# A fused block-sorted attention and max-out layer: Strassen's algorithm for the third item's hidden products, one-bank chains for the output groups, and a new order of all steps

## Chip, cores and metric

One core of a Trainium2 chip runs the kernel. The metric is the device time of one execution in microseconds. The profile shows one execution of its own; its span, from the first to the last instruction, is a little shorter than the device time.

## The reference

```python
B, H, S, D = 4, 8, 768, 64;  n_blocks = 8;  block = 96
P = sort_net                                   # (B, H, 8, 8)
for _ in range(5):
    P = np.exp(P - P.max(-1, keepdims=True))
    P = P / (P.sum(-1, keepdims=True) + 1e-09)
    P = P / (P.sum(-2, keepdims=True) + 1e-09)
k_sorted, v_sorted = P applied to the 8 blocks of k and of v
scores = q_b @ k_sorted_b.T / sqrt(D)          # within each block of 96
x = softmax(scores) @ v_sorted_b               # -> (B * S, H * D) = (3072, 512)
g = np.maximum(x @ w1, x @ w2)                 # w1, w2: (512, 1024)
out = g @ w_out                                # (3072, 512) float32
```

"Item" below is one of the four entries of the batch, 0 to 3 (768 tokens of x each).

## The kernel before

**Algebra.** max(a, b) = b + relu(a - b). So the kernel forms W1 - W2 once (in the place of W1, a quarter of its columns at a time), computes h = relu(x (W1 - W2)), and writes out = h W_out + x (W2 W_out). The product W2 W_out (512 x 512, in `wc`) is made once, from W2 transposed (`w2T`). Matmuls take bf16 and accumulate in float32.

**Stages per item.** Sort k (`sort_k`) and v (`sort_v`, `sort_v_pair` for items 1 and 2 together, `sort_v_halved`) by small matmuls on 64 rows of the array; transpose q; scores of 8 blocks at a time (`scores`, 64 rows, exponential on ScalarE into one of six buffers `e`); values (`values`, then a reciprocal and a multiplication on VectorE); transpose x (by matmul for item 0, by a transposing DMA on the SP queue for items 1 to 3); hidden products (`moe_h`, or `HGroup` with Strassen's algorithm); output products (`Group`).

**PSUM.** One pool of four tiles of two banks each. Every step that multiplies takes one of them; an output group holds its tile from its first to its last step.

**Hidden products.** For items 0 to 2, `moe_h` fills one tile per half of the tokens (`ch`) and quarter of the hidden columns (`t`): eight matmuls of 128 x 384 and one ReLU from PSUM, on ScalarE or VectorE. That is 64 matmuls per item; item 0's come in two halves of four (`ha`, `hb`). For item 3, two objects `HGroup` take half of the columns each and make seven products of four matmuls (Winograd's form of Strassen's algorithm): 56 matmuls. Their partial sums are kept in SBUF (steps 0, 2 and 3, a copy), or are added on VectorE (steps 1, 5 and 6) ahead of a ReLU from SBUF; step 4 is a ReLU from PSUM. The sums and differences of x that they need (`x_sums`, tokens X) are made for every item, since the output groups use them as well; those of the weights (`d_sums`, tokens Z, in the place of W2) are made once.

**Output products.** All items use seven products per group. `P` is the group of an item's first two tiles of 128 tokens in each half (12 matmuls of 128 x 256 per step), `U` that of the third tile (6 per step). Sums of g (`g_sums`, tokens G) and of W_out and W2 W_out (`weight_sums`, tokens w) come from VectorE. In `step`, items 0 to 2 alternate between the two banks of their tile: copies at steps 0 and 2, additions of PSUM and SBUF at steps 1, 3, 4, 5 and 6. Item 3 uses `chain`: steps 0, 2, 3 and 4 add up in bank 0 and are copied out after each, steps 1, 5 and 6 use bank 1 and end in additions.

**Order.** The kernel fixes the order of each engine's instructions itself: a list of tokens (`plan`) is run through `token`, and each token issues all its instructions at once, on whichever engines and queues they use. `s2.4` is the scores of item 2, unit 4; `v2.4` the values; `P1.3A` is step 3 of item 1's group P with the evacuation on ScalarE, `D` on VectorE, and `P` as a last letter on GpSimd; `Y3.0.5A` is step 5 of item 3's `HGroup` 0; `k`, `b`, `q`, `x`, `t` are sorting of k and v, transposes of q and x, and a re-ordering copy of v; `T`, `c` and `d` are W2's transposes, W2 W_out and W1 - W2; `lk`, `lq`, `lf`, `lv` load k, q and v through GpSimd's queue. Everything up to the first sorting of k stands ahead of the list: three pieces of v, three of k and four of q for item 0, the recurrence for P, and the weights' loads. Two small writes by GpSimd (`seen`) hold back the weights' loads until P and the first sorted k are there:

```python
    nc.gpsimd.tensor_copy(out=seen[0:G, 0], in_=p_bf[:, NB - 1, NB - 2 :])
    load_w_columns(w2_sb, moe_w2, 0, 1)
    ...
    nc.gpsimd.tensor_copy(out=seen[:, 1], in_=kT[0][:, 0:2])
    load_w_columns(w1_sb, moe_w1, 0, 1)
```

GpSimd's queue also computes two quarters of W1 - W2 (`d0P`, `d1P`), so loads that stand behind those in its order wait for them. At the start TensorE runs 92 matmuls on zeros, then more during the recurrence (`keep_streaming`). In the profile, lines 711 are `moe_h`, 779 `HGroup`, 934 the output products, 581 scores, 609 values, 960 additions, 967 and 969 copies of the output groups.

## Time and profile before

| | |
|---|---|
| device time, median of 3 runs | 159.38 us (159.37 to 160.71) |
| span of the profiled execution | 157.9 us |
| granted TensorE clock, mean | 1.000 |
| line 934, output products | 504 matmuls, 33% of the chain of waits |
| line 711, hidden products of items 0 to 2 | 192 matmuls, 20% of the chain |
| line 779, item 3's hidden products | 56 matmuls |
| exponentials, L597 | 32 on ScalarE, 808 ns each |
| multiplications after the values, L626 | 32 on VectorE, 687 ns each |
| ReLU of hidden products | 20 on ScalarE, 812 ns; 4 on VectorE, 951 ns |
| loads through GpSimd's queue | 13.37 MB written to SBUF, 48.3% of 16 engines' span |
| transposes of x and q, and stores, on hardware queues | 9.84 MB, 26.0% |

Each row of the profile's groups names the line, engine, operation, the tiles written and read, and the shapes; after the count come the total busy time, the mean duration of one in nanoseconds, and the idle time of the engine just before. Matmul durations overlap, so a product's pace is read from how long a run of them takes, not from its mean duration. "Chain of waits" is followed back from the last instruction, at each step to what released it.

### The profile page before, as it was taken

The page shows a single profiled execution, that of the slowest core. Times are in us where ns is not written, and L with a number is a line of the kernel's source. Part 1 is how long each engine was busy: PE and PEld are TensorE (multiplying, and loading weights), DVE is VectorE, ACT ScalarE, POOL GpSimd, SP SyncE. Part 2 cuts the span into 40 slices and gives each one's busy share as a digit, 9 for nine tenths or more (in the row PEclk, how much of TensorE's full clock was granted, in tenths as well). Part 3 has the DMA queues.
Part 4 walks back from the last instruction along what each step waited for, and adds up shares of the span by engine and source line. Part 5 has one row for each costly group of instructions (what it writes and reads, how often), then busy time and mean ns, then how long its engine had stood idle before and what let it go on. Part 6 is the DMA issues. An engine that isn't in the chain of part 4 may idle for free.

```text
span 157.9 us, 5185 instructions
## 1 busy us (share of the span) xinstructions
PE 149.7 (95%) x2260; PEld 115.1 (73%) x2264; DVE 127.1 (81%) x274; ACT 84.4 (53%) x111; POOL 29.3 (19%) x57
## 2 busy tenths in 40 slices
PE   6989799999999999999999999999999999999980
PEld 6839577756467788887676898766689886578870
DVE  4879799939969998892899989979878959799340
ACT  3489795656159993459148700793662106692010
POOL 7969997220100000004300000000000000000000
PEclk9999999999999999999999999999999999999999
DMA  2999999999999999795999995750020719000063
GB/s 40 192 204 199 186 202 205 214 214 216 213 203 217 214 145 192 261 132 174 143 220 211 138 147 115 238 215 0 4 50 4 111 42 395 0 4 0 18 254 129
DMA packets 28918, 23.93 MB, mean 152 GB/s; under 512 B 16672, under 2 KB 24608, under 8 KB 28896
## 3 DMA queue, kind: packets, MB, share of 16 engines
q0 software_dynamic: 9280, 13.37, 48.3%
q1 hardware_dynamic: 19200, 9.84, 26.0%
q8 instruction: 17, 0.28, 0.7%
q10 hardware_dynamic: 416, 0.39, 0.7%
q14 instruction: 5, 0.04, 0.1%
HBM read 26.75 MB, written 6.29 MB: 209 GB/s over the span
## 4 chain that ended last, share of the span: by engine, by line
PE 80%; DMA 9%; DVE 6%; issue 1%; POOL 0%; ACT 0%; DVEq 0%; POOLq 0%
PE out_ps L934 33%; PE h_ps L711 20%; DMA q_raw<-in_q_dram 6%; PE wc_ps L691 4%; PE o_ps L609 4%; DMA v_raw<-in_v_dram 3%; PE hb_ps L779 3%; DVE x L626 3%; PE s_ps L581 3%; PE hq_ps L779 2%; PE k_ps L486 2%; PE v_ps L551 2%; PE tw_ps L672 1%; PE tq_ps L453 1%; DVE o L960 1%
## 5 line engine op out<-in xcount | busy, mean ns | idle before, releaser
L711 PE MATMUL h_ps<-xT,w_sb 128*128 128x384 bf16 x192 | 33.9, 326 | 0.1
L597 ACT ACTIVATE e<-s_ps 96x768 bf16<-96x768 f32 x32 | 23.8, 808 | 13.3 <-PE s_ps L581 13.1
L711 PEld LDWEIGHTS <-w_sb 128*128 128x128 bf16 x192 | 17.8, 98 | 10.8
L725 ACT ACTIVATE g<-h_ps 128x768 bf16<-128x768 f32 x20 | 16.0, 812 | 15.1 <-PE h_ps L711 14.9
L626 DVE TENSOR_TENSOR x<-o_ps,rs 96x512 bf16<-96x512 f32 x32 | 22.0, 687 | 1.1
L934 PEld LDWEIGHTS <-g 128*128 128x128 bf16 x192 | 18.3, 98 | 2.3
L934 PEld LDWEIGHTS <-sums_g 128*128 128x128 bf16 x144 | 13.7, 98 | 1.7
L960 DVE TENSOR_TENSOR o<-out_ps,a 128x512 f32<-128x512 f32 (+1 forms) x20 | 11.0, 550 | 3.4 <-PE out_ps L934 2.1
L960 DVE TENSOR_TENSOR o<-out_ps,o 128x512 f32<-128x512 f32 (+1 forms) x16 | 8.8, 555 | 5.6 <-PE out_ps L934 5.5
L934 PE MATMUL out_ps<-wo_sb,g 128*128 128x256 bf16 x96 | 13.1, 273 | 0.0
L609 PEld LDWEIGHTS <-e 96*128 96x128 bf16 x256 | 10.8, 98 | 2.4 <-DVE x L626 0.2
L609 PE MATMUL o_ps<-v_sb,e 96*128 96x65 bf16 x256 | 12.1, 193 | 0.1
L934 PE MATMUL out_ps<-w2T,sums_x 128*128 128x256 bf16 x72 | 11.8, 273 | 0.0
L109 ACT CAST v_sb<-v_ps 96x1024 bf16<-96x1024 f32 x10 | 9.7, 1027 | 0.4 <-PE v_ps L528 0.4
L934 PEld LDWEIGHTS <-sums_x 128*128 128x128 bf16 x96 | 9.0, 98 | 1.2
L581 PE MATMUL s_ps<-qT,kT 64*128 64x96 bf16 x256 | 8.9, 204 | 0.7 <-issue 0.4
L620 DVE RECIPROCAL rs<-o_ps 96x8 f32<-96x8 f32 x32 | 6.3, 197 | 3.4 <-PE o_ps L609 3.2
L581 PEld LDWEIGHTS <-kT 64*128 64x128 bf16 x256 | 6.3, 94 | 3.6 <-issue 2.6
L109 ACT CAST kT<-k_ps 128x1024 bf16<-128x1024 f32 x7 | 7.0, 1013 | 3.4 <-PE k_ps L486 3.4
L969 ACT COPY o<-out_ps 128x512 f32<-128x512 f32 (+1 forms) x7 | 3.5, 503 | 9.7 <-PE out_ps L934 9.7
L111 DVE CAST v_sb<-v_ps 96x1024 bf16<-96x1024 f32 x6 | 7.3, 1216 | 1.2 <-PE v_ps L528 0.8
L779 PEld LDWEIGHTS <-w_sb 128*128 128x128 bf16 x56 | 5.5, 98 | 3.5
(135 smaller groups left out, 272.4 us busy)
## 6 DMA issues: line engine op xcount, KB each, us to landing
out_dram<-o SPq DMA_DIRECT2D x10, 512.0 KB, 3.3
v_raw<-in_v_dram POOLq DMA_DIRECT2D x8, 384.0 KB, 15.5
k_raw<-in_k_dram POOLq DMA_DIRECT2D x3, 768.0 KB, 19.3
w_sb<-in_moe_w_dram POOLq DMA_DIRECT2D x4, 256.0 KB, 6.3
w_sb<-in_moe_w_dram POOLq DMA_DIRECT2D x2, 512.0 KB, 9.0
wo_sb<-in_moe_w_out_dram POOLq DMA_DIRECT2D x2, 512.0 KB, 12.6
v_raw<-in_v_dram POOLq DMA_DIRECT2D x3, 256.0 KB, 5.4
k_raw<-in_k_dram POOLq DMA_DIRECT2D x3, 256.0 KB, 7.9
```

Source lines behind the costliest of these rows:

```text
L109: nc.scalar.copy(out=out_ap, in_=in_ap)
L111: nc.vector.tensor_copy(out=out_ap, in_=in_ap)
L581: nc.tensor.matmul(ps[:, h2 * 512 + ii * 128 : h2 * 512 + ii * 128 + BLK], kT[b][rows, (hp * 8 + i) * BLK : (hp * 8 + i) * BLK + 128], rhs ...
L597: nc.scalar.activation(out=e_out, in_=src, func=AF.Exp, scale=scale)
L609: nc.tensor.matmul(ps[:, h2 * 512 + ii * 65 : h2 * 512 + (ii + 1) * 65], e[:, (h2 * 4 + ii) * BLK : (h2 * 4 + ii) * BLK + 128], v_sb[:, m0 ...
L626: nc.vector.tensor_tensor(out=x, in0=ov[:, :, :, 0:D], in1=rs.to_broadcast([BLK, 2, 4, D]), op=ALU.mult,)
L691: nc.tensor.matmul(ps[:, 0:512], w2T[:, fb, dmt * 128 : (dmt + 1) * 128], wo_sb[:, fb, :], start=(fb == 0), stop=(fb == NFB - 1),)
L711: nc.tensor.matmul(h_ps[ch, t][:, m * 512 : m * 512 + TCH], w1_sb[:, hp, fb * 128 : (fb + 1) * 128], xT[:, b % 2, ch, hp % 2, hp // 2, :], ...
L725: nc.scalar.activation(out=g, in_=src, func=AF.Relu)
L779: nc.tensor.matmul(ps[:, m * 512 : m * 512 + TCH], w[:, k, c : c + 128], x[:, k], start=new and k == 0, stop=k == 1, skip_group_check=True,)
L934: ins = nc.tensor.matmul(self.ps[:, bank * 512 + p * NW : bank * 512 + (p + 1) * NW], left(self.b, lw, k, ti * 128), right(rw, k), start=n ...
L960: ins = nc.vector.tensor_tensor(out=self.part(ch, half), in0=self.by_tile(self.bank(n)), in1=other, op=ALU.add)
```

## The change

- Item 2's hidden products are made by two `HGroup`s, as item 3's. In the list, eight `h2` tokens give way to fourteen `Y2` tokens.
- All output groups use `chain`; the alternating form is gone. Items 0 to 2 store the first half of the tokens after step 4 and the second after step 6.
- All steps, those ahead of the list too, become tokens of one list, with a new order. `f` is filling on TensorE, `I` the identity, `lw`, `lk0`, `lq0` the pieces of item 0's v, k and q, `a` a load of weights (1: W1, 2: W2, by quarters of columns; 3: W_out, by halves), `S` a round of the recurrence, `m` masks, `g` and `J` selections, `D` the first block diagonals, `tv` the re-ordering of item 0's v. The weights' loads are no longer held back by the `seen` writes, and W1 and W2 come in seven pieces in another order, W_out between them.
- The buffers of the exponentials are handed out in the order in which they come free, not in turn.

```diff
...
@@ -177,24 +180,20 @@
     w2_sb = big.tile([128, HP, DFF], BF16, tag="w2", name="w2_sb")
     wo_sb = big.tile([128, NFB, DMODEL], BF16, tag="wo", name="wo_sb")
 
-    def load_w(dst, src):
+    def load_w(dst, src, i):
         s = src.rearrange("(t p) f -> p t f", p=128)
         n = s.shape[1] // 2
-        for i in range(2):
-            nc.gpsimd.dma_start(
-                out=dst[:, i * n : (i + 1) * n, :], in_=s[:, i * n : (i + 1) * n, :]
-            )
+        nc.gpsimd.dma_start(
+            out=dst[:, i * n : (i + 1) * n, :], in_=s[:, i * n : (i + 1) * n, :]
+        )
 
     def load_w_columns(dst, src, t0, t1):
         s = src.rearrange("(t p) f -> p t f", p=128)
         c = slice(t0 * DFF // 4, t1 * DFF // 4)
         nc.gpsimd.dma_start(out=dst[:, :, c], in_=s[:, :, c])
 
-    load_v(0, 3)
+    load_v(0, 3, which=0)
     ident = const.tile([128, 128], BF16, tag="ident", name="ident")
-    make_identity(nc, ident)
-    load_k(0)
-    load_q(0)
 
     id64 = const.tile([128, 64], FP32, tag="id64", name="id64")
     maskJ = const.tile([128, 7, NB], FP32, tag="maskJ", name="maskJ")
...
@@ -562,7 +563,7 @@
             eng=eng,
         )
 
-    e_tiles, x_tiles, e_next = {}, {}, [0]
+    e_tiles, x_tiles, e_free = {}, {}, list(e_bufs)
 
     def scores(b, u, n=0):
         ih, hp = divmod(u, HP)
...
-        e = e_bufs[e_next[0] % NE]
-        e_next[0] += 1
+        e = e_free.pop(0)
         src = ps[0:BLK].rearrange("p (t f) -> p t f", t=8)[:, :, 0:BLK]
         if b == 1:
             e_out = e[:, 0 : 8 * BLK].rearrange("p (t ch c) -> p t ch c", t=8, ch=2)
         e = e_tiles.pop((b, u))
+        e_free.append(e)
         m0 = (b % 2) * 64
         ps = ps_f32("o_ps")
         keep_streaming(ps, n)
@@ -991,21 +993,29 @@
             elif at == 4:
                 self.product(0, 4, "b22", False)
                 self.copy(self.part(0, 1), 0, eng)
-                self.store(0)
+                if last or len(self.tiles) > 1:
+                    self.store(0)
             elif at == 5:
                 self.product(1, 3, 3, True)
                 self.add(1, 1, 1, self.part(1, 1), [self.third], eng)
-                self.store(1, NW)
+                if last:
+                    self.store(1, NW)
             else:
                 self.product(1, "a22", 4, False)
                 self.add(1, 0, 1, self.part(1, 0), [self.second], eng)
-                self.store(1, 0, NW, nc.scalar)
+                if last:
+                    self.store(1, 0, NW, nc.scalar)
+                elif len(self.tiles) > 1:
+                    self.store(1)
+                else:
+                    nc.sync.dma_start(
+                        out=out[self.b * S : (self.b + 1) * S, :].rearrange(
+                            "(c t p) n -> p c t n", c=2, p=128
+                        )[:, :, self.tiles[0], :],
+                        in_=self.both,
+                    )
 
         def step(self, at, eng):
-            if at and self.b == B - 1:
-                self.chain(at, eng)
-                return
-            a = self.by_tile(self.a) if at else None
             if at == 0:
                 n = len(self.tiles)
                 self.ps = ps_f32("out_ps")
...
                 self.product(0, "a11", "b11", True)
                 self.first = self.copy(self.by_tile(self.a), 0, eng)
-            elif at == 1:
-                self.product(1, 2, 2, True)
-                self.second = self.add(1, 0, 1, a, [self.first], eng)
-            elif at == 2:
-                self.product(0, "a12", "b21", False)
-                self.copy(self.part(0, 0), 0, eng)
-            elif at == 3:
-                self.product(1, 1, 1, False)
-                self.third = self.add(0, 1, 1, a, [self.first], eng)
-            elif at == 4:
-                self.product(0, 3, 3, True)
-                self.fourth = self.add(1, 1, 0, self.part(0, 1), [self.third], eng)
-            elif at == 5:
-                self.product(1, 4, "b22", False)
-                self.fifth = self.add(0, 1, 1, a, [self.first, self.fourth], eng)
-                if len(self.tiles) > 1:
-                    self.store(0)
             else:
-                self.product(0, "a22", 4, False)
-                self.add(
-                    1, 0, 0, self.part(1, 0), [self.first, self.second, self.fifth], eng, True
-                )
-                if len(self.tiles) > 1:
-                    self.store(1)
-                else:
...
-
-    first, second, both = slice(0, 64), slice(64, 128), slice(0, 128)
+                self.chain(at, eng)
+
+    def spread_masks():
+        for c, n, m in [(2, 2, 0), (4, 3, 1)]:
+            nc.gpsimd.tensor_copy(
+                out=maskJ[:, c : c + n],
+                in_=maskJ[:, m].to_broadcast([128, NB, n]).transpose([0, 2, 1]),
+            )
+
+    first = slice(0, 64)
+    weights = {
+        1: (load_w_columns, w1_sb, moe_w1),
+        2: (load_w_columns, w2_sb, moe_w2),
+        3: (load_w, wo_sb, moe_w_out),
+    }
     keep_streaming(ps_f32("fill_ps"), 92 * 118, most=118)
-    for it in range(5):
-        sinkhorn(it)
-        if it < 3:
-            masks(it)
-        if it == 2:
-            turn_v(first, "A", 0, 18)
-        if it == 3:
-            turn_v(first, "A", 18, 36)
-    for c, n, m in [(2, 2, 0), (4, 3, 1)]:
-        nc.gpsimd.tensor_copy(
-            out=maskJ[:, c : c + n],
-            in_=maskJ[:, m].to_broadcast([128, NB, n]).transpose([0, 2, 1]),
-        )
-    turn_v(first, "A", 36, 56)
-    turn_v(first, "A", 56, 80)
-    block_diagonals_first()
-    seen = const.tile([128, 2, 2], BF16, tag="seen", name="seen")
-    nc.gpsimd.tensor_copy(out=seen[0:G, 0], in_=p_bf[:, NB - 1, NB - 2 :])
-    load_w_columns(w2_sb, moe_w2, 0, 1)
-    selections(1)
-    selections(2)
-    turn_v(first, "D", 80, 96)
-
-    sort_k(0, 0, 640, "A")
-    nc.gpsimd.tensor_copy(out=seen[:, 1], in_=kT[0][:, 0:2])
-    load_w_columns(w1_sb, moe_w1, 0, 1)
-    load_w_columns(w2_sb, moe_w2, 1, 2)
-    selections(3)
-    load_w_columns(w1_sb, moe_w1, 1, 2)
-    load_w_columns(w2_sb, moe_w2, 2, 4)
-    load_w_columns(w1_sb, moe_w1, 2, 4)
-    load_w(wo_sb, moe_w_out)
 
     def token(text):
 
...
@@ -1163,29 +1144,30 @@
     landed = const.tile([128, 4], BF16, tag="landed", name="landed")
     plan = [
         """
-        k0.1D k0.2A b0.2A b0.0D b0.3A q0.0D q0.1D s0.4 b0.1D s0.5 s0.6 s0.7 lk1 v0.4 s0.0 v0.6
-        s0.3 v0.5 d0P s0.1 T1D s0.2 d1P v0.7 x0.2A v0.1 T0A x0.3D ha0.1.0 v0.0 ha0.1.1 v0.2
-        hb0.1.1A lq1 v0.3 lf1 hb0.1.0A x0.0D T3D d3D T2A d2D x0.1A ha0.0.1 ha0.0.0 ha0.1.3
-        hb0.1.3A X0.1D X0.2D hb0.0.1A ha0.1.2 hb0.0.0A B0 ha0.0.2 hb0.1.2A w0.3D G0.0.1D w0.1D
-        hb0.0.2A c0A G0.0.2D X0.4D k1.0D k1.1A lf3 lf2 k1.2D X0.3D G0.1.1D c3D G0.1.2D c2D q1.0A
-        q1.1D c1A s1.4 w0.2D w1.1D lf0 G0.1.3D G0.0.3D s1.1 s1.2 ha0.0.3 hb0.0.3A t1.3D t1.2D
-        w1.2D P0.0A s1.3 t1.1D t1.0D s1.7 s1.6 G0.0.4D w0.4D P0.1D b2.1A G0.1.4D lq2 lk2 b2.3A
-        P0.2A p2.0D w1.3D b2.2D p2.1D b2.4A w1.4D b2.7A P0.3D q2.0 q2.1 b2.5A b2.6D b2.0A P0.4D
-        v1.4 v1.1 P0.5D s1.0 s1.5 v1.7 P0.6D v1.6 v1.5 U0.0A U0.1D k2.0A x1.2 k2.2A v1.0 U0.2A
-        x1.3 v1.2 U0.3D x1.0 v1.3 k2.1A lk3 k3.2D U0.4D s2.7 s2.3 s2.6 U0.5D x1.1 U0.6D s2.2
-        s2.5 s2.0 h1.1.1A v2.7 h1.1.3D v2.3 v2.0 y1 h1.0.1D h1.1.2D h1.1.0A G1.1.1D lq3 v2.6
-        k3.0D G1.0.1D k3.1A G1.1.3D h1.0.0A G1.0.2D h1.0.2A lv0 G1.0.3D s2.4 p3.0A s2.1 X1.1D
-        P1.0A p3.1D q3.0 X1.2D h1.0.3A G1.0.4D G1.1.2D q3.1 X1.3D Z1D x2.3 X1.4D v2.5 P1.1D lv1
-        U1.0A v2.1 P1.2D v2.4 P1.3D G1.1.4D P1.4D U1.1D v2.2 t3.0D U1.2D U1.3D t3.1D x2.2 x2.1
-        P1.5D U1.4D t3.2D s3.4 s3.5 x2.0 P1.6D s3.7 s3.3 t3.3D U1.5D U1.6D b3.0A b3.1D s3.2
-        h2.1.3A b3.2D Z2D b3.3A h2.1.0A X2.1D X2.2D h2.1.1D G2.1.1D Z4D X2.4D h2.1.2A v3.3
-        G2.0.1D v3.4 h2.0.0A h2.0.1A G2.1.2D h2.0.3A v3.2 x3.1 v3.7 h2.0.2A G2.0.2D v3.5 P2.0A
-        X2.3D s3.1 G2.1.4D s3.0 s3.6 P2.1D U2.0D U2.1D v3.6 G2.1.3D v3.0 G2.0.3D x3.3 U2.2D
-        P2.2A x3.2 U2.3D v3.1 Z3D P2.3D G2.0.4D x3.0 P2.4D U2.4D U2.5D P2.5D P2.6D U2.6D X3.1D
-        X3.2D X3.3D Y3.1.0A Y3.0.0A Y3.1.1D Y3.1.2A Y3.0.2A X3.4D Y3.0.1D Y3.1.3A Y3.0.3A
-        Y3.0.5A Y3.1.5D Y3.1.4A Y3.0.4A Y3.0.6A Y3.1.6A G3.0.1D G3.0.2D G3.1.1D G3.1.2D P3.0A
-        U3.0D P3.1D P3.2A G3.1.4D G3.0.3D G3.0.4D U3.1D U3.2A G3.1.3D P3.3D P3.5D U3.3A P3.4A
-        P3.6D U3.5D U3.4D U3.6D
+        f4 lw1 I1 lk0.0 S0 m0 S1 lw2 m1 lk0.2 lk0.1 lq0.0 S2 m2 J1 tv0.18A S3 tv36.56A S4 tv56.80A
+        lq0.1 D0 tv18.36A tv80.96D k0.0A lq0.3 k0.2D k0.1A lq0.2 b0.3D b0.1A q0.0D g1 a1.0.1 a2.0.1
+        a2.2.3 m3 b0.0A b0.2D s0.5 q0.1D s0.1 s0.4 v0.5 s0.7 v0.1 s0.6 v0.4 s0.0 a2.1.2 a1.2.4 v0.7
+        s0.3 T0D x0.2A v0.6 s0.2 a2.3.4 T2D T1A a3.1 v0.0 x0.3D d0P ha0.1.0 d2D a3.0 v0.3 d3D x0.0A
+        lf1 g3 X0.1D hb0.1.0A ha0.1.2 hb0.1.2A v0.2 g2 B0 a1.1.2 lk1 ha0.0.0 ha0.1.3 x0.1A T3D
+        G0.0.1D hb0.1.3D lq1 X0.3D X0.2D lf2 ha0.0.2 c3D w0.1D X0.4D d1P c0D w0.3D c2D ha0.0.1
+        hb0.0.0D hb0.0.2D ha0.1.1 hb0.1.1A hb0.0.1D k1.0A k1.2A k1.1A q1.0A G0.1.1D G0.0.2D G0.1.2D
+        lf0 G0.0.4D G0.0.3D q1.1D c1A w0.2D ha0.0.3 t1.0D s1.1 G0.1.3D lf3 s1.2 t1.1D s1.3 hb0.0.3D
+        t1.3D lq2 w1.1D P0.0A s1.6 s1.5 s1.4 t1.2D w1.2D lk3 P0.1D b2.1D w1.3D p2.0D b2.5A P0.2A
+        b2.7A b2.6D b2.4A w0.4D P0.3A b2.2A G0.1.4D b2.3A b2.0D P0.5D P0.4A p2.1D w1.4D lk2 v1.4
+        q2.0 v1.5 P0.6D U0.0A q2.1 v1.3 x1.2 s1.7 s1.0 Z1D U0.1D k2.1A v1.7 U0.2A v1.6 v1.0 v1.2
+        U0.3A x1.3 U0.5D x1.1 k2.2A k2.0A v1.1 x1.0 U0.4A U0.6D s2.3 s2.4 s2.5 h1.1.2A h1.1.0D X1.1D
+        s2.1 s2.6 X1.3D X1.2D h1.1.3A y1 v2.4 v2.3 Z3D h1.1.1A G1.1.1D Z2D k3.2A s2.7 X1.4D G1.0.1D
+        lv0 Z4D s2.2 h1.0.0A lq3 lv1 h1.0.1D v2.5 G1.0.2D G1.1.2D h1.0.2A G1.0.3D U1.0A v2.1 v2.2
+        h1.0.3A G1.1.3D U1.2A v2.6 U1.1D p3.0A k3.1A G1.0.4D k3.0D s2.0 p3.1D U1.3A U1.5D q3.0
+        G1.1.4D v2.7 q3.1 P1.0A t3.0D U1.4D x2.3 x2.1 t3.1D U1.6D t3.2D v2.0 t3.3D P1.2A P1.1D x2.0
+        x2.2 P1.3A s3.7 b3.0D b3.1A P1.4A s3.0 b3.2D b3.3A P1.5D Y2.0.0A X2.1D s3.6 X2.2D X2.3D s3.2
+        X2.4D P1.6D Y2.0.2A Y2.0.1D s3.3 v3.7 Y2.0.3A Y2.0.5D Y2.1.0A v3.2 Y2.0.4A Y2.0.6D Y2.1.2A
+        Y2.1.1D s3.4 v3.3 Y2.1.3A Y2.1.5A U2.0A v3.6 Y2.1.4A G2.0.1D Y2.1.6A G2.0.3D G2.0.2D P2.0A
+        s3.1 G2.1.1D s3.5 G2.1.2D G2.1.3D U2.1D x3.1 x3.3 P2.1D v3.4 U2.2A G2.1.4D G2.0.4D P2.2A
+        v3.1 v3.0 x3.0 U2.3A U2.5D U2.4A v3.5 x3.2 U2.6D P2.3D P2.5D X3.1D Y3.1.0A X3.2D Y3.0.0A
+        Y3.0.1A P2.4A P2.6D X3.3D X3.4D Y3.0.2A Y3.1.2A Y3.1.1D Y3.0.3A Y3.1.3A Y3.0.5A Y3.0.4D
+        Y3.1.5D Y3.1.4A Y3.0.6A U3.0A Y3.1.6A G3.0.1D G3.0.2D G3.1.1D P3.0A G3.1.2D G3.0.3D G3.1.3D
+        G3.0.4D P3.1D P3.2A U3.2A U3.1D G3.1.4D U3.3A P3.3D P3.5D P3.4A P3.6D U3.5D U3.4A U3.6D
         """,
     ]
     for part in plan:

```

## Prediction

> **What bounds the kernel now.** I read the page first, then the chain of waits in order of time, then busy time by stretch, then the groups by shape.
>
> ```profile
> span 157.9 us, 5185 instructions
> ...
> PE 149.7 (95%) x2260; PEld 115.1 (73%) x2264; DVE 127.1 (81%) x274; ACT 84.4 (53%) x111; POOL 29.3 (19%) x57
> ...
> DMA  2999999999999999795999995750020719000063
> ```
>
> TensorE is busy 95% of the span. The DMA engines are full for about the first 50 us and have room after that.
>
> ```profile
> 7.59 8.98 DMA q_raw<-in_q_dram
> 16.61 0.55 PE tq_ps L433 x12
> ...
> 48.80 1.31 PE out_ps L934 x12
> 50.11 0.62 PE s_ps L581 x24
> 50.72 1.42 PE out_ps L934 x12
> ...
> 139.61 13.86 PE out_ps L934 x126
> 153.50 0.42 DVE o L960
> ```
>
> The columns are start, duration and what. The chain waits for the last part of item 0's q until 16.6, is nearly all TensorE from there to 153.5, and ends with one addition and a store (4.4 us to 157.9). Two prices come from here. Twelve output products take 1.31 us, but 1.42 where they follow a score or sorting product (64 rows instead of 128): each change between the two kinds costs about 0.1 us. And item 3's output groups, which already accumulate in one bank, ran 126 products in 13.86 us, 0.110 each, so they lost next to nothing.
>
> ```profile
> 11.50:24.50 13.00, 11.70 (x350) 9.87 (x349) 11.48 (x21) 11.42 (x15) 12.72 (x20) 1.00 1.33 196
> 24.50:46.40 21.90, 21.74 (x338) 13.85 (x339) 17.55 (x35) 10.91 (x13) 4.61 (x8) 1.00 1.11 212
> 90.00:130.50 40.50, 40.50 (x498) 32.44 (x495) 34.67 (x68) 14.81 (x20) 0.00 (x0) 1.00 0.44 97
> 130.50:139.60 9.10, 9.10 (x59) 5.51 (x57) 7.85 (x14) 6.48 (x9) 0.00 (x0) 1.00 0.42 163
> 139.60:153.50 13.90, 13.86 (x127) 12.09 (x124) 9.43 (x19) 4.35 (x8) 0.00 (x0) 1.00 0.18 66
> ```
>
> After each stretch and its length stand PE, PEld, DVE, ACT and POOL, then clock, DMA share and GB/s. TensorE has holes only before 24.5. From 46.4 on a product saved is time saved, if VectorE (86% in 90 to 130.5) and ScalarE keep up.
>
> ```profile
> L711 PE MATMUL h_ps<-xT,w_sb 128*128 128x384 bf16 x192 | 33.9, 326 | 0.1
> L779 PE MATMUL hb_ps<-sums_x,w_sb 128*128 128x384 bf16 x24 | 4.4, 326 | 0.0
> L798 DVE TENSOR_TENSOR g<-hq_ps,hs 128x768 bf16<-128x768 f32 x4 | 3.6, 953 | 0.9 <-ACT hs L791 0.8 <-PE hq_ps L779 0.2
> L969 ACT COPY o<-out_ps 128x512 f32<-128x512 f32 x4 | 2.4, 597 | 6.1 <-PE out_ps L934 6.1
> L960 DVE TENSOR_TENSOR o<-out_ps,a 128x512 f32<-128x512 f32 x10 | 6.8, 683 | 2.1 <-ACT e L597 1.2 <-PE out_ps L934 0.9
> ```
>
> The mean of a product (326 ns) counts its way through the array; the pace is 8 in 1.30 us in the chain, 0.163 each.
>
> **Item 2's hidden products.** Eight groups of eight products (64) become two Strassen groups of 28 (56): 8 x 0.163 = **1.30 us** less on TensorE, in a stretch without holes. Evacuation grows. Gone are seven ReLUs on ScalarE (7 x 0.81) and one on VectorE (0.95). New are six copies (0.80) and two ReLUs (0.80) from PSUM on ScalarE, six additions on VectorE (0.95, L798), four ReLUs on VectorE (0.36, L802) and two on ScalarE (0.84, L800). ScalarE goes from 5.7 to 8.1 us, VectorE from 0.95 to 7.2. The sums of x and weights that the products read were already made for items 2 and 3.
>
> Around them VectorE has, by my count over the new list from Y2.0.6 to U2.1, 9.5 us of work against 8.3 of TensorE; the stretch before it has 7.8 against 8.6. The cover is that earlier slack and the 4.2 us of other products between the last hidden product (Y2.1.6) and the first that reads its sums (U2.2). Without the cover the cost is 9.5 - 8.3 = 1.2; I take 0.2.
>
> **Output groups of items 0 to 2 in one chain.** Their 378 products stay (0.109 each). Of seven evacuations per group, steps 3 and 4 turn from additions into copies, which ScalarE can take. Counting letters in the lists, items 0 to 2 go from 16 wide and 18 narrow evacuations on VectorE (0.69 and 0.42) to 10 and 10: 18.6 to 11.1 us. ScalarE goes from 5 and 3 (0.59 and 0.37) to 11 and 11: 4.1 to 10.6. With item 2's hidden work VectorE is about even and ScalarE gains some 9 us on 84, so neither becomes the bound on average.
>
> The price is waits. Before, a product returned to a bank two steps later, and the lists put 0.9 to 5.3 us of other products between. Now step 3 waits for the copy of step 2, step 4 for that of step 3 and step 6 for the addition of step 5. The closest pairs in the new list have between them: U2 steps 3 to 4, 0.66 us; U0 steps 2 to 3, 0.73; P1 steps 3 to 4, 0.82; U2 steps 5 to 6, 0.90; P0 steps 2 to 3, 0.99; P1 steps 5 to 6, 1.10. The need is a copy (0.37 or 0.59), or an addition (0.42 or 0.69), and some 0.2 of handing over: 0.6 to 0.9. The nearest row is U3 steps 5 to 6 in the trace before: 0.66 between, one addition ahead in VectorE's queue, and TensorE waited 0.09 at 152.4. Six such waits give 0.5, and only half the pairs are as tight: I take **0.3**, with 0 and, if each finds one full evacuation ahead (0.8, an exponential), 6 x 0.8 = 4.8 as ends. Behind a waiting product stands everything on TensorE. [...]
>
> **The list.** Over the whole list the changes between 64-row and 128-row products rise from 51 to 55, 33 to 35 of them after item 1's first scores: **+0.2** there, the other two inside the front below.
>
> In the front the order of loads changes: weights follow q at once (two writes by GpSimd that held them back are gone), w_out now stands before the second quarter of W1, and the masks and selections move among the loads. The recurrence that ends with p at 11.1 us is unchanged, and so is the place of k and q in the queue (2.36 MB at about 0.2 MB per us, last q near 16.5). New is that only half of q is needed for the first three scores: q's first half is evacuated near 16.4 instead of 16.87, its scores follow, and the values' VectorE work can start near 18.7 instead of 19.78. That is a gain of 1.1 us at 19. By the first hidden product it is 0.4 in time (24.1 for 24.48) plus 0.7 of products done earlier.
>
> Part of it is lost again, because two steps then need late loads. Before the second quarter of W1 come 2.36 MB of v, k and q, 1.57 MB of W1 and W2, 1.05 of w_out and 0.39 of v; with its own 0.26 it lands at about 35. GpSimd's difference d1P (2.15, L233) then ends near 37.0, and ha0.0.1 is due on TensorE at 36.7. Behind d1P on GpSimd wait five loads, of which v's pieces are due on VectorE only after 46. Item 1's q lands near 42.4, due 42.6. I take 0.3 of waits, so item 1's first scores stand at 46.75 with 0.65 us more work done than at 46.4 before: **-0.3**, bounds -0.9 (nothing waits) and +0.7 (both loads a microsecond later; the first delay then hides the second). [...]
>
> Of the older waits after 46.4 (holes of 0.1 to 0.3 us beside the changes of kind, about 0.9 in all) the new list may lose some; I take -0.3, ends -0.9 and 0. The end (U3.5, U3.4, U3.6, last addition, store) is as before: 4.4 us.
>
> **Sum.** -1.30 + 0.2 + 0.3 + 0.2 - 0.3 - 0.3 = -1.2: the span goes from 157.9 to 156.7. The median of the runs, 159.38, is 1.48 above the span, which I keep: **158.2 us**. The forecast's own band is 157.2 to 159.2.
>
> **Rivals.** *The single bank* (slower): chain waits find ScalarE's queue full. For: from item 1's first scores to P0.3 the new list gives ScalarE 9.5 us beside 8.9 of TensorE, and P0.2 to P0.4 stand among sorting copies of 1.0 each. Against: the list before had 10.7 beside 8.2 there without losing more than 0.6. It decides from 1.2 us beyond my 0.3, about 0.25 per tight pair; at 4.8 instead of 0.3 the time is 162.7, at half of it 160.3.
>
> *The loads*: the front gives back its gain, +0.7 instead of -0.3: 159.2. For: the DMA engines are full there. Against: bytes up to item 1 are the same.
>
> *Not what it says*: VectorE in item 2's stretch takes back the saved 1.3 (1.2 instead of 0.2, and nothing from older waits): 158.2 + 1.0 + 0.3 = 159.5. For: 9.5 against 8.3. Against: item 3's same steps ran with no hole.
>
> *Everything fits*: front -0.9, chain 0, older waits -0.9, item 2 0: -1.3 + 0.2 - 0.9 - 0.9 = -2.9, so 156.5.
>
> **Chances.** One per cent (157.8 and 161.0) is about what a measurement of this kernel can tell from no change, as its three runs spread 0.8%. Forecast 0.46 (0.16 of it under 157.8), everything fits 0.27 (all under), loads or item 2 0.11 (within), single bank 0.16 (0.13 above 161.0, 0.03 within). Faster 0.16 + 0.27 = 0.43; within 0.30 + 0.11 + 0.03 = 0.44; slower 0.13. Range 156.7 to 160.6: it leaves out the far end of everything fits (about 0.05) and of the single bank (about 0.14).
>
> **What would show it.** L711 falls to 128 products and L779 rises to 112, at 0.163. Right: item 2's stretch and the output groups show 12 products in 1.31 to 1.42 and no waits named out_ps from L960 or L969 over 0.3 us; first hidden product near 24.1, item 1's first scores near 46.8, last product near 152.3. Wrong: holes before wide or narrow output products among sorting copies (single bank); TensorE waiting for w_sb, L233 or q_raw between 31 and 44 (loads); idle TensorE with VectorE solid in item 2's stretch.

## The result, and the profile after

The changed kernel takes 164.67 us (median of 4 runs, 164.12 to 167.66) where the kernel before takes 159.52 in the same job: 1.029 times, with a 95% interval of 1.023 to 1.034. It is slower, by about 5 us where 1.2 less were predicted. The ratio leaves out the run of 167.66, in which the granted clock was lower in stretches (0.979 in the mean), and unless it is said otherwise the readings below are of another execution (e0 below), span 161.8, clock 1.00.

The page's totals and its groups, to be held against those of before:

```profile
PE 150.6 (93%) x2253; PEld 115.6 (71%) x2256; DVE 128.9 (80%) x270; ACT 92.0 (57%) x127; POOL 29.3 (18%) x56
...
DMA  3999999999999920999799839993022062700046
...
L712 PE MATMUL h_ps<-xT,w_sb 128*128 128x384 bf16 x128 | 23.1, 326 | 1.8 <-DMA xT<-x 1.4
L970 ACT COPY o<-out_ps 128x256 f32<-128x256 f32 (+1 forms) x21 | 10.0, 474 | 18.3 <-PE out_ps L935 16.7
```

The edit did what it says: 128 ordinary hidden products are left of 192, and the output groups' evacuations have moved to ScalarE (84.4 to 92.0 us busy). TensorE's busy share fell from 95 to 93%, though it has less to do, and the DMA row has a new gap in its 15th and 16th slice (2 and 0, 56.6 to 64.7 us; 9 and 9 stood there before). What TensorE waits for from 46.4 on, in us in total, times and longest:

```profile
PE h_ps L712 <- DMA xT<-x: 1.4, 1, 1.4
PE tq_ps L454 <- issue: 1.4, 1, 1.4
PE hb_ps L780 <- DMA xT<-x: 1.0, 1, 1.0
PE out_ps L935 <- ACT e L597: 0.3, 1, 0.3
```

(The second began at 45.5 and ended inside the stretch.) None is an output product waiting for an addition or a copy. Two are the transposes of x by DMA. The chain of waits, in order of time, shows how they hang together (start, duration, what):

```profile
45.52 1.36 issue
...
73.19 3.92 DMA xT<-x
...
80.24 10.68 DMA v_dc<-in_q_dram
...
91.70 1.47 ACT q_pair L413
...
102.03 5.07 DMA xT<-x
```

Item 1's x is transposed late; GpSimd's small copy of it (token y1) holds v3's pieces and q3's load; q3 lands at 90.9, is rearranged, is transposed on SyncE, and only behind that come x's transposes for item 2, for which its hidden products wait. (Between 93 and 102 the listed chain follows ScalarE and TensorE. The last part of item 2's x was computed by 100.5; SyncE was with x's first two transposes until 101.3 and with a store until 101.9, and took up the last two at 102.0.) SyncE's timeline shows the queue, first in the kernel before, then here:

```profile
56.62 3.86 SPq L422 DMA_TRANSPOSE qT<-q_pair  x2
...
65.50 5.67 SPq L639 DMA_TRANSPOSE xT<-x  x4
...
87.38 4.12 SPq L422 DMA_TRANSPOSE qT<-q_pair  x2
91.59 5.90 SPq L639 DMA_TRANSPOSE xT<-x  x3
```

```profile
63.60 0.41 SPq L975 DMA_DIRECT2D out_dram<-o  x1
64.11 1.81 SPq L423 DMA_TRANSPOSE qT<-q_pair  x1
65.98 1.13 SPq L975 DMA_DIRECT2D out_dram<-o  x1
67.16 2.49 SPq L423 DMA_TRANSPOSE qT<-q_pair  x1
69.69 6.95 SPq L640 DMA_TRANSPOSE xT<-x  x4
...
94.57 3.30 SPq L423 DMA_TRANSPOSE qT<-q_pair  x2
97.98 3.32 SPq L640 DMA_TRANSPOSE xT<-x  x2
```

In this execution a transposing DMA holds SyncE for 1.2 to 2.5 us. Before, q2's two went at 56.6 to 60.5; now they start 7.5 us later (its second rearrangement, p2.1, runs on VectorE at 62.4 instead of 56.0), and SyncE works almost without a pause from 63.6 to 77.3.

To find where the 5 us arise I counted, for each execution, the matmuls that had started by a time, each at the pace of its shape (distance to the next: an output product 0.109, a hidden product 0.163; the small ones, scores and transposes among them, some hundredths), fill left out. The table has this work done, less that of before, in us. The paces of the small products can be taken in more than one way, which moves the entries by some 0.2, and a few matmul records are missing (at most 4 in 2260).

```
by time (us)         24.5   46.4     73     78    104    108    115    150
e0  changed          -1.3   -2.3   -2.0   -3.8   -4.3   -5.4   -5.6   -6.1
e6  front of before  -0.5   -0.4   -1.6   -2.5   -2.3   -3.4   -3.9   -4.1
e9  q3 load ahead     0.0    0.2   -0.6   -0.8   -1.1   -1.9   -2.4   -2.8
e10 x2 early         -0.2    0.4    0.4    0.2    0.6    0.2    0.1   -0.2
e11 x2 early, plain   0.2    0.7    1.2    1.1    1.1    0.7    0.6    0.2
e5  before, chain     0.2    0.1   -1.4   -1.6   -5.7   -6.8   -6.4   -9.7
```

(The other rows are experiments below.) In the changed kernel 2.3 us are lost up to 46.4, where it stands in the middle of the stop in item 1's q transposes (45.5 to 46.9); at 47.0, behind the stop, it is 2.7. Of these 0.7 come back by 73, 1.8 go between 73 and 78, 1.1 between 104 and 108, and 1.2 in small pieces. Against that stand 1.3 us of products fewer: 6.1 - 1.3 = 4.8, about the 5.0 us by which the last product is late (158.2 for 153.2).

### The profile page after: what moved, and what is told of

Read it like the earlier page. It is cut to its first block, busy times and chain, and to the rows that moved or that the text cites. A ratio compares the mean times of both kernels' runs of the same rounds, so it can differ in the third digit from the quotient of the medians.

```text
span 165.8 us, 5166 instructions
## 1 busy us (share of the span) xinstructions
PE 152.5 (92%) x2253; PEld 115.3 (70%) x2256; DVE 129.4 (78%) x270; ACT 91.8 (55%) x127; POOL 29.5 (18%) x56
## 4 chain that ended last, share of the span: by engine, by line
PE 73%; DMA 11%; DVE 8%; issue 3%; POOL 2%; ACT 1%; POOLq 0%
PE out_ps L935 32%; PE h_ps L712 10%; PE hb_ps L780 7%; DMA xT<-x 6%; DMA k_raw<-in_k_dram 5%; PE hq_ps L780 5%; PE o_ps L610 4%; PE s_ps L582 4%; PE k_ps L487 4%; PE wc_ps L692 2%; DVE wt_early L853 1%; ACT e L597 1%; PE v_ps L552 1%; PE v_ps L508 1%; DVE sums_x L865 1%
## 5 line engine op out<-in xcount | busy, mean ns | idle before, releaser
L597 ACT ACTIVATE e<-s_ps 96x768 bf16<-96x768 f32 x32 | 24.4, 806 | 2.8 <-PE s_ps L582 2.4
L712 PE MATMUL h_ps<-xT,w_sb 128*128 128x384 bf16 x128 | 23.5, 329 | 2.2 <-DMA xT<-x 1.4
L970 ACT COPY o<-out_ps 128x256 f32<-128x256 f32 (+1 forms) x21 | 10.0, 474 | 18.4 <-PE out_ps L935 16.7
L712 PEld LDWEIGHTS <-w_sb 128*128 128x128 bf16 x128 | 12.0, 99 | 10.6 <-issue 3.7
L780 PEld LDWEIGHTS <-w_sb 128*128 128x128 bf16 x112 | 10.7, 99 | 9.0 <-DMA xT<-x 2.6
L726 ACT ACTIVATE g<-h_ps 128x768 bf16<-128x768 f32 x9 | 7.3, 812 | 15.8 <-PE h_ps L712 15.8
L728 DVE TENSOR_SCALAR g<-h_ps 128x768 bf16<-128x768 f32 x7 | 6.6, 955 | 7.5 <-PE h_ps L712 7.5
L109 ACT CAST kT<-k_ps 128x1024 bf16<-128x1024 f32 x10 | 9.7, 1013 | 1.4 <-PE k_ps L487 1.4
L111 DVE CAST v_sb<-v_ps 96x1024 bf16<-96x1024 f32 x7 | 8.5, 1218 | 2.0 <-PE v_ps L529 1.7
L780 PE MATMUL hb_ps<-sums_x,w_sb 128*128 128x384 bf16 x48 | 9.4, 326 | 0.0
L109 ACT CAST v_sb<-v_ps 96x1024 bf16<-96x1024 f32 x9 | 8.9, 1019 | 0.3 <-PE v_ps L508 0.3
```

Source lines behind the costliest of these rows:

```text
L109: nc.scalar.copy(out=out_ap, in_=in_ap)
L111: nc.vector.tensor_copy(out=out_ap, in_=in_ap)
L597: nc.scalar.activation(out=e_out, in_=src, func=AF.Exp, scale=scale)
L712: nc.tensor.matmul(h_ps[ch, t][:, m * 512 : m * 512 + TCH], w1_sb[:, hp, fb * 128 : (fb + 1) * 128], xT[:, b % 2, ch, hp % 2, hp // 2, :], ...
L726: nc.scalar.activation(out=g, in_=src, func=AF.Relu)
L780: nc.tensor.matmul(ps[:, m * 512 : m * 512 + TCH], w[:, k, c : c + 128], x[:, k], start=new and k == 0, stop=k == 1, skip_group_check=True,)
```

## The experiments

All ratios are against runs of the kernel before in the same job; the span is that of the profiled execution. A hole of TensorE is given below from the start of one product to the start of the next, less the pace of the first; the lists of waits count from the modelled end of a product, and so have some 0.2 less.

```
run                   median us   ratio  95% interval     span
e0 changed, again       163.49   1.0250  1.0165-1.0335   161.8
e1 c1 between           163.93   1.0252  1.0214-1.0290   161.5
e2 q2 first             163.49   1.0211  1.0158-1.0265   161.5
e3 U stores on ScalarE  166.39   1.0396  1.0337-1.0454   163.4
e4 item 2 plain         166.26   1.0363  1.0285-1.0442   164.9
e5 before, chain        168.64   1.0515  1.0455-1.0576   166.6
e6 front of before      161.56   1.0110  1.0020-1.0200   159.4
e7 DMA order            176.95   1.0984  1.0875-1.1092   174.8
e8 q2 early             160.76   1.0044  1.0004-1.0083   159.5
e9 q3 load ahead        160.69   1.0062  1.0025-1.0100   158.8
e10 x2 early            158.36   0.9929  0.9896-0.9962   156.1
e11 x2 early, plain     159.26   0.9979  0.9955-1.0003   157.0
f1 weights held         163.68   1.0189  1.0087-1.0291   162.0
f2 W1 ahead of w_out    164.59   1.0263  1.0198-1.0327   162.2
```

**The changed kernel again** (e0), no edit:

> The changed kernel as it is, for a second profile. If the time goes where its first profile has it, TensorE shows the same four holes: before the hidden products near 38 us (0.8), inside item 1's transposes of q near 45 (1.9), before item 1's hidden products near 75 (1.8), and before item 2's near 107 (2.5), with TensorE at half its pace for about 3 us behind one or more of the long ones. If it were the chains in one bank, holes of 0.1 to 0.8 us would stand before output products (line 935) all through 53 to 135. Time 164 to 165 us.

It is the base for what follows. The four holes are there, somewhat shorter than in the first execution (0.44, 1.53, 1.58 and 0.25, 1.19 us), and the half pace that the expectation names is not.

**A w product between item 1's k and q** (e1):

```diff
- k1.0A k1.2A k1.1A q1.0A ... q1.1D c1A w0.2D
+ k1.0A k1.2A k1.1A c1A q1.0A ... q1.1D w0.2D
```

> One step of W2 W_out (token c1) is moved from behind item 1's q transposes to between its k sorting and its q transposes. [...] With eight wide products (1.7 us, 32 instructions) in between, the hole shrinks from 1.9 to under 0.4 us, the half pace behind it goes, and the time falls by 1.5 to 3.5 us, to 161 to 163. Rival, q of item 1 comes late: the transposes go on at the same moment as before (46.9 us), the hole only moves in front of them, and the time stays within 0.5 us of 164.4.

The hole of 1.53 us inside q1's transposes shrank to 0.23, and the scores after them then waited 0.95 for VectorE's copy of q1. By 50 us TensorE was some 0.7 us further than in e0, by 78 only some 0.3, and the time is the same: what was won in front was waited for at x's transposes. Why TensorE stops at this place no run shows.

**q2's transposes a few steps earlier** (e2):

```diff
- b2.0D P0.5D P0.4A p2.1D w1.4D lk2 v1.4 q2.0 v1.5 P0.6D U0.0A q2.1 v1.3
+ b2.0D p2.1D q2.0 q2.1 P0.5D P0.4A w1.4D lk2 v1.4 v1.5 P0.6D U0.0A v1.3
```

> Item 2's second pairing copy and its two q transposes (p2.1, q2.0, q2.1) are moved ahead of P0.5 and P0.4, so that they stand on the SP queue before item 0's two stores instead of between and behind them. Theory: SP takes 1.3 to 3.0 us for each transposing DMA and works in order, so item 1's x transposes were held up by it, not by their data; the hole before item 1's hidden products near 75 us falls from 1.8 to under 0.5 us and the time by 1 to 2 us. Rival, the values on VectorE are what x waits for: the hole stays at 1.5 us or more and the time within 0.5 us.

The wait ahead of item 1's hidden products fell from 1.58 and 0.25 us to 0.47, the one ahead of item 2's rose from 1.19 to 1.98. The chain's first link moved; its last, q3 and x2, stayed where they were.

**U's stores on ScalarE's queue** (e3):

```diff
- nc.sync.dma_start(
+ nc.scalar.dma_start(
      out=out[self.b * S : (self.b + 1) * S, :]...
```

> The 512 KB store of each U group of items 0 to 2 is issued on ScalarE's queue instead of SP's. Theory: item 1's U store stands on SP directly before item 2's third x transpose (103.5 and 104.1 us) and moves ahead of it in the same ring, so that this transpose lands 5.4 us after its issue instead of 3.0. Without it the hole before item 2's hidden products near 107 falls from 2.5 to under 0.7 us, the half pace behind it goes, and the time falls by 2 to 3.5 us, to 161 to 162.5. Rival, x of item 2 is late because its last values are: the hole stays over 2 us and the time within 0.5 us.

Slower. SyncE went straight from q3's transposes to all four of x2's, and they ended at 106.4 all the same (105.1 in e0); the holes grew in sum (1.41 and 0.67; 1.98). So it is not the store between x2's transposes that makes them late. Why it lost another 1.6 us of span I did not follow up.

**Item 2's hidden products in ordinary groups** (e4); Strassen's third use is undone, all else stays:

```diff
- Y2.0.0A ... Y2.0.2A Y2.0.1D ... Y2.0.3A Y2.0.5D Y2.1.0A ... (14 steps)
+ h2.0.0A ... h2.0.2A ... h2.1.0A h2.1.2D h2.0.1A ... (8 groups)
```

> Item 2's hidden products go back to eight ordinary groups of eight; everything else as changed. TensorE then has 1.3 us more of products (8 x 0.163) and VectorE and ScalarE have less to evacuate. If Strassen's saving is real and the loss lies in the waits ahead (x and q transposes, front), the waits stay and the saving goes: about 1.0 to 1.3 us slower than the changed kernel, some 164.7. If the new evacuations had eaten the saving, the time is the changed kernel's within 0.3 us or below it, 163.2 to 163.7. If the wait for x's transposes is what counts in that stretch, the wait before item 2's hidden products stays between 1 and 2.5 us in both.

The wait for x2 stayed (1.50 us) and the products added came on top, which speaks for a real saving and a loss that lies elsewhere. Its size is better read from e10 and e11, since e4's execution also had TensorE at half pace for 3.4 us (granted clock 0.5 from 48.2 to 51.6) after the hole in q1's transposes (1.89 here).

**The kernel before, with the one-bank chain alone** (e5), its own list and letters (the conditions on the stores inside `chain`, as in the changed kernel, are left out here):

```diff
-            if at and self.b == B - 1:
+            if at:
                 self.chain(at, eng)
```

> The kernel before with its own list; only the output groups of items 0 to 2 follow the one-bank chain, engine letters as they stood (steps 3 and 4 become copies on the same engine). If the chain's waits cost little, as the changed kernel's trace has it (no hole before output products above 0.5 us), the time is 159.5 to 161.0. If the single bank is the cause (rival), the list that leaves less between the chained steps shows it: 162 or more, with TensorE waiting for out_ps from the addition's or copy's line.

The rival's end, 8.8 us slower, and with the rival's mark. TensorE's waits from 46.4 on:

```profile
PE out_ps L934 <- DVE o L967: 4.9, 5, 1.6
PE out_ps L934 <- DVE o L960: 2.1, 4, 0.8
PE out_ps L934 <- ACT o L969: 0.6, 1, 0.6
PE out_ps L934 <- ACT g L725: 0.6, 1, 0.6
```

Of these 8.2 us, 7.6 are waits for copies and additions of the output groups (`o`), 0.6 is one for a ReLU (`g`). The old list puts one chained step behind the next; the new list does not, and shows none of these waits. So the chain needs its list: my forecast that its waits are cheap held for this list, not for the chain.

**The front of before** (e6): loads, selections and steps of before up to item 1's first scores but one, then the changed list less what is done.

```diff
- f4 lw1 I1 lk0.0 S0 m0 S1 lw2 ... a3.1 ... a1.1.2 lk1 ... lf0 G0.0.4D
+ (list of before, up to) lf0 G0.1.3D G0.0.3D
  s1.1 ...
```

> The list of before up to item 1's first scores but one (46 us there), loads and selections as before; after that the changed list, less what is already done. By the work that TensorE had done at 46.4 us the changed front is about 2.9 us behind. If TensorE's work binds from there on, this gains 2.5 to 3 us: 160.5 to 161. If the middle is bound by the chain q2's rearrangement, transposes on SyncE, loads of q3, transposes of x (each waiting for the one before), the gain is only as much as that chain starts earlier: 161.5 to 163, with the waits before item 1's and item 2's hidden products as long as or longer than before (1.5 and 1.2 us).

The front is worth 1.9 us of median (the two jobs' ratios give 2.2, the two profiled spans 2.4). Of the 2.3 us of work gained behind the stop, at 47, 2.0 are left at 150; the waits at 72.0 (1.60 and 0.25), 92.5 (0.44) and 106.5 (0.92) stay.

**q2 and q3 early in the changed kernel** (e7), q3's load as soon as its place is free:

```diff
- p2.0D b2.5A ... b2.0D P0.5D P0.4A p2.1D w1.4D lk2 ... h1.0.0A lq3 lv1
+ p2.0D p2.1D q2.0 q2.1 b2.5A ... b2.0D lq3 P0.5D P0.4A w1.4D lk2 ... h1.0.0A lv1
```

> Changed kernel; q2's second rearrangement and its transposes right after the first (about 4 us earlier on VectorE), and q3's load issued as soon as its place is free, instead of behind the wait for item 1's x and q2's transposes and behind a piece of v3. If the chain x1's transposes, q3's load, q3's rearrangement, q3's transposes, x2's transposes makes the two holes at 73.8 (1.58 and 0.25) and 105.8 (1.19) and the one at 94.4 (0.47), 2 to 3.3 us go: 160.5 to 161.5. If the 16 DMA engines are simply full there, the transposes get longer beside q3's load and the time stays within 0.7 us of 163.5.

A mistake of placing. GpSimd stood at q3's load until 62.3, and behind it stood k2's load, due on TensorE at 68.4: a hole of 9.6 us (k_raw, issued at 63.21, landed at 78.03). It says nothing of the rest.

**q2 early, with the front of before** (e8):

```diff
- p2.0D b2.5A ... P0.4A p2.1D w1.4D lk2 v1.4 q2.0 v1.5 P0.6D U0.0A q2.1
+ p2.0D p2.1D q2.0 q2.1 b2.5A ... P0.4A w1.4D lk2 v1.4 v1.5 P0.6D U0.0A
```

> The kernel with the front of before (161.56 us), and q2's second rearrangement with both transposes of q2 right after the first rearrangement, instead of some 5 us later; no load is moved. If the wait before item 1's hidden products (1.60 and 0.25 us at 72 to 74) is the queue on SyncE (q2's transposes, then x's, each 1.2 to 3 us of issue), it goes: q2's transposes start near 57 instead of 62.3, and 1.5 to 2 us are gained: about 159.7; item 1's x landing earlier lets v3 and q3 load earlier, so the wait before item 2's hidden products (0.92) shrinks too, if that chain is what makes it. If x's transposes are slow only because the DMA engines are full then, they start earlier and end as late as before: 161.3 to 161.8.

The wait ahead of item 1's hidden products is gone. x's transposes started 2.9 us earlier than in e6 (65.1 for 68.0) but took 9.0 us instead of 6.9, so GpSimd's loads behind them moved by 0.9 only, and the wait ahead of item 2's hidden products rose to 1.69. Half of each expectation held.

**q3's load ahead of v3's, and cover for x2** (e9):

```diff
- lv0 Z4D s2.2 h1.0.0A lq3 lv1
+ lq3 Z4D s2.2 h1.0.0A lv0 lv1
- P1.5D Y2.0.0A X2.1D s3.6 X2.2D X2.3D s3.2 X2.4D P1.6D Y2.0.2A Y2.0.1D
+ P1.5D s3.6 P1.6D Y2.0.0A X2.1D X2.2D s3.2 X2.3D X2.4D Y2.0.1D Y2.0.2A
```

> As the run with q2 early, and besides q3's load ahead of v3's first piece on GpSimd, and item 1's last output products (12, 1.3 us) ahead of item 2's first hidden products instead of behind them. By the chain q3's load, its rearrangement on ScalarE, its transposes, x2's transposes on SyncE, the 0.44 at 92.5 and the 0.92 at 106.5 go: 1.0 to 1.4 us less than the run with q2 early, about 158.4, which is below the kernel before (159.8). If TensorE's waits there come from VectorE (v3's turning, sums of x), not from the transposes, nothing is gained: 159.5 to 160.

No gain in time. The waits at 98.8 and 103.3 (0.27, 1.69) became 0.74 at 102.9, where P1.6 stands one score behind P1.5 and waits for its addition (the tight pair is mine), and 0.42 twice, where item 2's products wait for sums of x that VectorE could form only when x2 was there.

**x2 early** (e10):

```diff
- U1.0A v2.1 v2.2 h1.0.3A G1.1.3D U1.2A v2.6 U1.1D p3.0A ... p3.1D U1.3A U1.5D q3.0
-   G1.1.4D v2.7 q3.1 P1.0A t3.0D U1.4D x2.3 x2.1 ... v2.0 t3.3D P1.2A P1.1D x2.0 x2.2
+ U1.0A v2.1 v2.2 p3.0A h1.0.3A G1.1.3D U1.2A v2.6 p3.1D x2.1 x2.2 q3.0 q3.1 U1.1D ...
+   U1.3A U1.5D G1.1.4D v2.7 P1.0A x2.3 t3.0D U1.4D v2.0 ... x2.0 t3.3D P1.2A P1.1D
- P1.5D s3.6 P1.6D Y2.0.0A X2.1D X2.2D
+ P1.5D Y2.0.0A X2.1D s3.6 X2.2D P1.6D
- hb0.0.3D
+ hb0.0.3A
```

> As the run with q3's load ahead, and besides: q3 is rearranged ahead of item 1's last hidden product, x2's transposes for head pairs 1 and 2 go ahead of q3's on SyncE, those for 3 and 0 follow 2 to 3 us earlier than now, item 2's first hidden product stands between the last two output steps of item 1 (instead of scores alone), and the last ReLU of item 0 goes from VectorE to ScalarE. By the chain (x2 lands near 105, sums of x on VectorE at 105.8 to 106.9, hidden products wait 0.42 twice; the last two output steps wait 0.74), 1.0 to 1.6 us go: 159.1 to 159.7, below the kernel before by 0 to 0.5 us in that job's pairs. If VectorE and ScalarE bind between 98 and 112 by their work and not by the time at which x2 lands, the holes move and the time stays at 160.2 to 160.8.

158.36 us, 0.7% below the kernel before (interval 0.4 to 1.0%): a small gain, but clear of zero. The last part of the edit moves products and one evacuation too, so the step from e9 to e10 is not one of SyncE's queue alone. TensorE has no wait left after 46.4 that the profile lists. Its stretches (length, then PE, PEld, DVE, ACT, POOL, clock, DMA share, GB/s), of the changed kernel and of this one:

```profile
24.50:46.40 21.90, 20.69 (x300) 13.49 (x299) 20.47 (x40) 8.64 (x11) 8.28 (x14) 1.00 1.14 211
90.00:130.50 40.50, 39.17 (x546) 30.66 (x544) 35.35 (x67) 24.64 (x36) 0.00 (x0) 1.00 0.51 102
```

```profile
24.50:46.40 21.90, 21.90 (x343) 13.93 (x341) 17.54 (x35) 11.05 (x13) 4.54 (x8) 1.00 1.11 212
90.00:130.50 40.50, 40.50 (x490) 31.59 (x488) 35.00 (x65) 22.02 (x33) 0.00 (x0) 1.00 0.43 107
```

Both stretches are full. On SyncE q2's transposes now start at 55.75 and two of x2's stand ahead of q3's:

```profile
55.75 4.73 SPq L423 DMA_TRANSPOSE qT<-q_pair  x2
...
86.86 3.83 SPq L640 DMA_TRANSPOSE xT<-x  x2
90.80 4.08 SPq L423 DMA_TRANSPOSE qT<-q_pair  x2
```

**The same with item 2 plain** (e11), the edit of e4 in e10's list:

> As the run with x2 early, but item 2's hidden products in eight ordinary groups (64 products instead of 56). Where no transfer hides it, the Strassen groups of item 2 are worth 8 x 0.163 = 1.3 us: this run is 1.0 to 1.4 us slower than its partner. If their evacuations (six additions, four ReLUs on VectorE, eight copies and ReLUs on ScalarE) take the saving back, the two are within 0.4 us.

0.90 us slower in the median, 0.9 in the two profiled spans. Between the two 1.30 us of products lie (56 for 64). The plain one is 0.4 ahead in work at 150, but it is 0.4 ahead at 24.5 already, where the two programs are the same: no loss to evacuation shows. The spans of all runs say the same: their medians are 156.0 and 157.4, 1.4 apart. The device time has 0.5 less of a difference because it exceeds the span by 2.3 us in e10 (and in e9) and by 1.8 in e11 and in the kernel before; what lies outside the span no profile here shows. And the plain one is the kernel before within its interval: chain and list together, once the waits are mended, are worth about nothing, and the gain is Strassen's.

**The weights held until p and k are there** (f1):

```diff
- g1 a1.0.1 a2.0.1 a2.2.3 m3
+ g1 m3 z0 a1.0.1 z1 a2.0.1 a2.2.3
```

(z0 and z1 are the two small writes of before.)

> Changed kernel; the masks' spreading goes ahead of the first weight loads on GpSimd, and the two small writes are put back that hold the first weight load until p is there and the next two until k's first third is sorted. If weights moving beside k and q are what makes the front late, k's last third no longer lands at 13.85 but near 13.3, the first scores follow at 17.1 instead of 17.5, and by 20 us TensorE has 0.5 us more work done than in the changed kernel; of the total 0.3 to 0.8 us is left (162.7 to 163.2). If the front is late for other reasons (the order of k, v and q steps, the fills), nothing changes at 17.5, and the later weights cost up to 0.5 us: 163.5 to 164.

The idea fell: with one weight load at 11.4 and the rest from 15.2 on, k's last third was sorted at 14.32, later than in e0 (13.88), and the first scores came at 17.90. The weights beside k and q are not why the front is late.

**W1's second quarter ahead of w_out** (f2):

```diff
- a2.3.4 T2D T1A a3.1 ... d2D a3.0 ... B0 a1.1.2 lk1
+ a1.1.2 a2.3.4 T2D T1A ... d2D a3.1 ... x0.0A a3.0 ... B0 lk1
```

> Changed kernel; the second quarter of W1 is loaded ahead of w_out's halves, which go two and three places later. If the late quarter makes the hole, GpSimd's difference d1P runs before 32 instead of 35.4 to 37.6, the hole at 38.6 (0.44) and the slow two-input operation of VectorE beside it (2.28 us) go, and what waited behind d1P on GpSimd (v, q2, k loads) is issued 3 to 5 us earlier: 0.5 to 1.5 us less, 162.0 to 163.0. If w_out is then the late one, the products of w_out and w2 (216 ns each, from 33.6) wait instead, and the time is 163.5 or more.

Each sign came, the gain did not. GpSimd's difference moved from 35.4 to 27.4, the hole at 38.6 went, q2's load was issued at 33.45 instead of 38.56, and VectorE's subtraction that had run beside the difference took its usual time. In e0, and then here:

```profile
36.14 1.96 DVE L853 TENSOR_TENSOR wt_early<-wo_sb 128x1024 bf16<-128x1024 bf16 x1
```

```profile
37.01 0.68 DVE L853 TENSOR_TENSOR wt_early<-wo_sb 128x1024 bf16<-128x1024 bf16 x1
```

But another wait opened at 31.2 (0.59), the work done by 46.4 rose by 0.2 only, and the waits at 74.1 (1.36) and 105.4 (2.04) took it.

## Why the prediction was wrong, step by step

**The step that failed is the list.** The prediction priced the front at -0.3 (bounds -0.9 and +0.7), older waits at -0.3, and gave SyncE's queue no term at all. The front cost some 2 us instead, and the queue some 2.9; the older waits no run separates.

- *The front.* It had lost 2.7 us of work by 47, almost four times the far bound, and undoing it gives some 2 us (e6). The premise was that only half of q is needed for the first scores, so that they come earlier. That half was to be evacuated near 16.4 and was at 17.4, and the scores came at 17.49 instead of 17.07:

```profile
17.07 0.34 PE L581 MATMUL s_ps<-qT,kT 64*128 64x96 bf16 x8
```

```profile
17.49 0.34 PE L582 MATMUL s_ps<-qT,kT 64*128 64x96 bf16 x8
```

  VectorE still copies v's first part and then q's, as before, and all of it stands 0.4 to 0.6 us later: the first product with p starts at 11.51 instead of 11.16, and k's last third was waited for 0.45 us before 13.88. Then the first values stopped for 1.0 us (19.4 to 20.3, "issue"). The rival "the loads" had the right place (w_sb and GpSimd's difference at 35 to 38), but it is a small part: the hole there is 0.44 us, at 38.6, behind a VectorE subtraction that took 1.3 us longer beside that difference, and f2 takes it away without effect on the time. Another 1.5 us of the front is the hole in q1's transposes, which the new list puts right behind k1's sorting, where 15 wide products stood between; it was in neither forecast nor rival. Which of the front's steps makes the 1.3 us by 24.5 stays open; the weights beside k and q are excluded (f1).
- *SyncE's queue, not priced.* I checked the copies and products that the list moves, and not the transposing DMAs that p, q and x tokens issue. q2's rearrangement moved 6.4 us back, and with it both of its transposes, x1's behind them, GpSimd's wait for x1, q3's load, and x2's transposes. That is 1.8 us at 73 to 78 and 1.1 at 104 to 108. Mending single links (e2, e8, e9) moved the wait to the next; mending all of them, with a few products moved besides (e10), took it away. From e6 to e10 the ratio falls from 1.011 to 0.993, which is 2.9 us.
- *Strassen's third use.* Right in mechanism, and nearly in size: -1.30 of products, and a price in evacuation put at 0.2 of which the spans of e10 and e11 (1.4 apart) show nothing. In device time it is -0.9 where -1.1 stood, and the rest lies outside the span. The rival "not what it says", in which VectorE takes the saving back, is not borne out.
- *The one-bank chain.* Right for this list: +0.3 was forecast, and one wait of an output product, 0.3 long, is listed (for an exponential). Its far end, 4.8, was reckoned for the new list's six tight pairs; on the old list the chain costs 8.8 (e5). That the list was laid anew is what pays for the chain.
- *"Everything fits"* (156.5) was not reached either. Mended, the idea measures 158.36, with the predicted 158.2 beside it. That agreement is luck: the forecast was for another list, and its front was wrong.
- *The 1.48 kept from span to median.* It set a median beside the span of another execution; run by run the device time exceeds the span by about 1.9, in the kernel before and in the changed one. It is a small part of the error.
- *The signs named.* Hidden products 128 and 112 at 0.163: right. First hidden product near 24.1: 26.4. First scores of item 1 near 46.8: 50.4. Last product near 152.3: 158.2.

Of the two rivals that end later than the forecast by way of waits, the loads were a small part of it and the single bank none.

## What to carry to other kernels

When a list or schedule is laid anew, follow the transfers as carefully as the products: for each queue write down what is issued, in order, behind what it waits, and who waits for it; a transpose by DMA that moves 6 us back can carry a load, a second transpose and a whole stage with it. An algorithm that saves products shows its gain only where no transfer ends the wait, so compare it with its plain form on a list without holes. And put a load ahead of another on one queue only if its place is free by then (e7: a hole of 9.6 us).

## What the runs showed of the hardware

**Holes at a fixed place in TensorE's program.** Inside runs of small matmuls TensorE stopped with nothing to wait for ("issue" in the chain above). Counting matmuls and weight loads from the start, such stops lie at 700 to 704 in fourteen of the sixteen profiles (0.4 us at 18.6 in the kernel before, 0.6 at 18.9 in the first execution of the changed one, 1.0 at 19.4 in e0) and at 1466 to 1469 in nine (1.9 us in the first execution and in e4). They last 0.2 to 2.0 us. The page counts transfers under the name "instruction":

```profile
q8 instruction: 17, 0.28, 0.7%
```

Each is 16 KB (0.28 MB by 17), and in e0 two of them ran from 17.9 to 18.9 and from 44.0 to 45.2, just ahead of the stops at 19.4 and 45.5; in the first execution from 17.2 to 18.1 and from 44.1 to 45.3, beside stops at 18.9 and 45.2. Behind most of the 17 no stop follows, and what makes one is not shown. e1, which put eight products of 0.22 us ahead of it, made the stop 0.23. In the kernel before and in e10 the counts from 1466 on also fall inside item 1's q transposes, but 15 and 16 such products stand between them and the k sorting, and there is no stop; the changed list has the two side by side.

**Half pace after short holes, and without them.** After holes of 1.88 and 2.48 us (first execution), 1.89 (e4), 2.03 and 2.23 (e7) the granted clock was 0.5 for 3.4 us (512 columns in 0.427 us instead of 0.216); after others of 1.98 (e2 and e3) and 2.04 (f2) it stayed at 1.0. But it also fell to 0.5 for 3.4 us at 21.6 in e8 and at 22.7 in f1, where no hole of the 5 us before was over 0.7 us; in e0, with a hole of 1.1 us among the same small matmuls (19.4), it did not. What decides it stays open.

**GpSimd beside VectorE.** A subtraction of two SBUF inputs on VectorE took 1.96 us in e0 (2.36 in the first execution) beside GpSimd's difference of weights, 0.68 elsewhere, and 0.68 when f2 moved the difference away: 1.3 to 1.7 us more for one instruction.
